# Strassen-type products inside the first MLP stage of an attention and MLP kernel on one Trainium2 core

## The chip, the cores and the metric

The kernel runs on one core of one Trainium2 chip. The metric is the device time of one execution in microseconds. The core's engines that matter here: TensorE (PE in the profile, with its weight loads as PEld), VectorE (DVE), ScalarE (ACT), GpSimd (POOL) and SyncE (SP), whose queue starts most of the DMA transfers. TensorE's results go to PSUM banks; everything else that it reads lies in SBUF.

## What is computed

```
q, k, v: (4, 8, 768, 64) float32; proj (64, 6); w_in (512, 2048); w_out (2048, 512); alpha (2048)

bucket = sum((x @ proj > 0) * 2**bit)                  # for q and for k
mask   = q_bucket[..., :, None] == k_bucket[..., None, :]
scores = where(mask, q @ k.T / 8, -1e9)
attn   = softmax(scores) @ v                           # (4, 8, 768, 64)
x = attn.transpose(0, 2, 1, 3).reshape(3072, 512)
h = x @ w_in
g = maximum(h, 0) + alpha * minimum(h, 0)
out = g @ w_out                                        # (3072, 512) float32
```

## The kernel before

The kernel first runs the attention of all 16 pairs of heads, and then, batch by batch, the MLP: for each of the four batches a first stage (w_in and the activation) and a second stage (w_out). All matrix products of the MLP are float32, and TensorE makes each of them in two passes, so that a product over one block of 128 rows of K is two entries in the trace.

**Seven products in place of eight.** The first stage of a batch computes the transpose of h, 2048 rows (features) by 768 columns (tokens), as a product of w_in's transpose with x's transpose. It is split in two along the features, along K (2 x 256) and along the tokens (2 x 384 columns; `CW` is 384), and the resulting 2x2 by 2x2 product is made with seven partial products (Strassen's method, in Winograd's form) over sums and differences of quarters. The sums of w_in's quarters were made during the attention and lie in DRAM as `w_in_s`: for each block i seven matrices m = 0 to 6, of two K blocks each. The sums of x's quarters are `x_m[b, 0..6]`, of which 3, 5, 4 and 6 are made by VectorE from the loaded quarters 0, 1, 2 and 5 (`sum_x`, 128x768 each).

**A block.** `ff1(b, i)`, i = 0 to 7, makes 128 features of each feature half: a `Product` with seven steps. Step n multiplies one of the seven matrices with one of the seven x's, into one of three PSUM banks a, b, c:

| step | matrices (w, x) | bank | what follows |
|---|---|---|---|
| 1 | 0, 0 | a, new | ScalarE copies a into bank b (the seed of b; in block 0 into SBUF as `p1`) |
| 2, 22 | 1, 1 | b, adds to the seed | quarter "11" is done: ScalarE copies it into SBUF as `h`, VectorE applies the activation |
| 5 | 3, 3 | c, new | ScalarE keeps c as `p5` |
| 6 | 4, 4 | a, adds | ScalarE keeps a as `u1` |
| 3 | 6, 2 | c, new | VectorE adds `u1` and c: quarter "12", activation |
| 7 | 5, 5 | a, adds | ScalarE keeps a as `u2`; VectorE adds `p5` and `u2`: quarter "22", activation |
| 4 | 2, 6 | a, adds | quarter "21": ScalarE copies it as `h`, VectorE applies the activation and makes four differences of g |

Each of those products is two matrix multiplications of 128x128 by 128x384 (two K blocks). Banks a come from `two_banks`, three buffers of two banks each that all stages share in turn; b and c are one bank each. Step 1 of the next block is put before step 4 of the present one, so the order on TensorE is, for block i: 1 of i, 4 of i-1, 2, 5, 6, 3, 7, then 1 of i+1.

**The second stage** (`ff2`) is built the same way with two levels: seven outer products n (in the order 1, 2, 5, 6, 3, 7, 4), each of them a `Product` of seven with 192 columns (`HC`) and four K blocks. VectorE makes the inner sums of w_out (`sum_w2`, tiles ws3 to ws6 from the loaded tile `wl`) and of g (`sum_g2`, tiles gs3 to gs6) as they are needed. The outer products are added up in the tiles m, m1 and m5, turned by VectorE (`turn_out`, two transposes each) and stored by twelve DMAs on SyncE's queue.

**Order.** `do` (`keep_in_program_order`) lets every computing instruction stand on its engine where the code has it; the DMAs that aren't pinned may be placed earlier. The loop over `blocks` runs through the batches: eight blocks of the first stage, seven of the second. In it, `load_w` asks for the first stage's matrices three blocks ahead, `load_x` and `sum_x` prepare the next batch's x during the second stage (the sums in its last block, n = 6), and `largest` and `verdict`, a check of the value ranges, run in the first stage of batch 1.

**Where a wait arises.** Dependencies between engines are kept by tile. A buffer that is given out again waits for all that used it before, and a two-bank tile counts as one tile.

Of the kernel before, what the change touches and what calls it, by code (L numbers as in the profile page):

```python
# [8 lines left out]
F32 = mybir.dt.float32  # L9
# [398 lines left out]
def fast_path(  # L408
# [13 lines left out]
    P = 128  # L422
# [52 lines left out]
    w_out_r = dram.tile([4, P, NI, DM // 2], F32, name="w_out_r")  # L475
    w_out_s = dram.tile([4, P, NI, DM // 2], F32, name="w_out_s")
    x_s = dram.tile([B, NP, P, S], F32, name="x_s")
    NW = NK * NF // 2
    wmax = const.tile([P, NW], F32, name="wmax")

# [216 lines left out]
    def two_banks(name):  # L697
        return psum.tile([P, 2, 512], F32, name=name, tag="sc", bufs=3)
# [167 lines left out]


    x_m, w_m, g_m = {}, {}, {}

    def pinned(when, ins):  # L870

# [90 lines left out]
                self.finish("21", self.ps["a"], None)  # L962

    def ff1(b, i):
        def finish(c, t, more):
            if more is None:
                h = mid.tile([P, CW], F32, name=f"h{b}_{i}", tag="h")
                do(ACT.copy(h, t))  # L968
            else:
                h = t  # L970
                do(DVE.tensor_tensor(h, t, more, op=ALU.add))

            al = alpha[:, i + NI * (c[0] == "2") :][:, :1]
            m = {"11": 0, "21": 1, "22": 2, "12": 5}[c]
            do(DVE.scalar_tensor_tensor(new_g(b, m)[:, i], h, al, h, op0=ALU.mult, op1=ALU.max))  # L975
            if c == "21":

                for to, x, y in ((3, 5, 0), (5, 2, 5), (4, 2, 3), (6, 1, 4)):
                    do(DVE.tensor_tensor(new_g(b, to)[:, i], g_m[b, x][:, i], g_m[b, y][:, i], op=ALU.subtract))  # L979

        w = w_m[b * NI + i]
        return Product(
            f"f{b}_{i}", CW, 2, lambda m, k: w[:, m, k], lambda m, k: x_m[b, m][:, k], finish,
            seeded=("b",) if i else (),
        )

    def new_g(b, m):

# [7 lines left out]
    H2, HK, HC = DM // 4, NI // 2, CW // 2  # L996
    w2, g2, m2, to_turn = {}, {}, {}, []

    def load_w2(b, n):
# [289 lines left out]
    for j, (b, what, n) in enumerate(blocks):  # L1289
        n2 = n + 1 if what == "2" else 0 if n == NI - 1 else 7  # L1290
        if n2 == 0:
            sides_g(b, 0)
            sum_w2(b, 0, 3, 4)
        now.step(2) if j else now.step(6)
        if j == 0:
            now.step(3)
            now.step(7)
            now.step(2)
        now.step(22)
        if (b, what, n) == (1, "1", 1):  # L1300
# [21 lines left out]
        if what == "1":  # L1322
            load_w(b * NI + n + 3)

            if 0 <= n - NI + (4 if b else 2) < 2:
                load_w2(b, n - NI + (4 if b else 2))
        else:
            load_w2(b, n + 2)
            if b + 1 < B:
                if n == 0:  # L1330
                    load_x(b + 1)
                if n == 6:
                    for m in range(4):
                        sum_x(b + 1, m, DVE)
        if j + 1 < len(blocks):
            turn_out()
        else:
# [38 lines left out]
```

## Time and profile before

| | |
|---|---|
| runs | 868.88, 869.24, 870.54 us; median 869.24 |
| profiled execution | 869.49 us, its span (first to last instruction) 867.7 us |
| busy in the span | PE 857.9, DVE 732.7, ACT 377.5, POOL 115.2 us |
| granted TensorE clock | 0.998 |
| attention and what lies before the MLP | to about 312 us |
| first stage of batches 1, 2, 3 | about 449 to 514, 587 to 652, 724 to 789 us |
| DMA | 135.4 MB, mean 156 GB/s |

The batches are counted from 0, as in the code. "Busy" counts the time in which at least one instruction of the engine runs, by the profile; the ends of matrix multiplications are modelled, and a row of several in a line of the timeline gives the start of the first and the time to the end of the last. In such rows the numbers of buffers and batches are left out: `f_3a` is bank a of block 3 in whichever batch, `z_4a` bank a of the second stage's outer product 4. What stands in brackets is the idle time before an instruction and what ended it. The page's part for the chain that ended last is empty for this kernel.

### The profile page before, as it was taken

Reading aid. Unit: us, or ns where it says so; the run is one execution under the profiler, and the core shown is the slowest. Engines: PE = TensorE matmul, PEld = TensorE weight load, DVE = VectorE, ACT = ScalarE, POOL = GpSimd, SP = SyncE. Lnnn points to the kernel's source line nnn. Section 1 sums busy time; section 2 is a strip of 40 time slices with the busy share of each in tenths; the row PEclk is TensorE's granted clock in tenths of the full one; section 3 lists DMA queues with packets and bytes.
Section 4 is the critical chain, followed back from the end, with each engine's and each line's share of the span. In section 5 each row is a group of like instructions: output and inputs, shape, how many; then the busy total and the mean of one; then the engine's idle time right before and its main releaser. Section 6 shows DMA issues by size and latency. Waiting matters only on the chain.

```text
span 867.7 us, 14629 instructions
## 1 busy us (share of the span) xinstructions
PE 857.9 (99%) x5458; PEld 572.7 (66%) x5458; DVE 732.7 (84%) x1188; ACT 377.5 (44%) x682; POOL 115.2 (13%) x249
## 2 busy tenths in 40 slices
PE   9999999999999999999999999999999999999996
PEld 4444444444444445569985559996558997557996
DVE  6999999999999977899887669897669898668886
ACT  7777888877788823321113331112332112232111
POOL 1322423432433310210000000000000000000001
PEclk9999999999999999999999999999999999999999
DMA  8956879778697536775334444433425334420242
GB/s 204 189 130 134 209 179 232 173 200 235 132 265 198 158 131 235 258 280 191 116 115 122 138 153 133 144 127 90 173 86 182 129 108 130 149 85 1 97 164 60
DMA packets 171105, 135.36 MB, mean 156 GB/s; under 512 B 126240, under 2 KB 155088, under 8 KB 167440
## 3 DMA queue, kind: packets, MB, share of 16 engines
q1 hardware_dynamic: 158528, 108.44, 44.1%
q0 software_dynamic: 9488, 24.56, 9.5%
q10 hardware_dynamic: 3008, 1.33, 0.6%
q8 instruction: 45, 0.74, 0.4%
q14 instruction: 36, 0.29, 0.1%
HBM read 104.87 MB, written 28.31 MB: 153 GB/s over the span
## 4 chain that ended last, share of the span: by engine, by line


## 5 line engine op out<-in xcount | busy, mean ns | idle before, releaser
L786 PE MATMUL sc<-qT,kT 64*128 64x384 f32 x768 | 155.3, 483 | 0.0
L789 ACT ACTIVATE pt<-sc 128x768 f32<-128x768 f32 x192 | 153.9, 812 | 3.1 <-PE sc L786 2.8
L819 PE MATMUL av<-pt,vn 128*32 128x385 f32 (+1 forms) x1536 | 127.0, 486 | 0.0
L819 PEld LDWEIGHTS av<-pt,vn 128*32 128x32 f32 x1536 | 50.3, 109 | 73.8 <-issue 68.8
L786 PEld LDWEIGHTS sc<-qT,kT 64*128 64x128 f32 x768 | 68.5, 187 | 37.6 <-issue 37.3
L979 DVE TENSOR_TENSOR g<-g,g 128x384 f32<-128x384 f32 x128 | 68.3, 554 | 2.2
L1098 POOL DMA_DIRECT2D out_dram<-o x4 | 2.2, 555 | 474.2 <-DVE o L1091 474.2
L786 PE MATMUL sc<-qb,kb 64*128 64x384 bf16 x384 | 63.5, 324 | 0.5 <-ACT pt L789 0.3
L975 DVE SCALAR_TENSOR_TENSOR g<-h,alpha 128x384 f32<-128x384 f32 x60 | 36.8, 614 | 25.2 <-ACT h L968 25.1
L1036 DVE TENSOR_TENSOR ws<-wl 128x512 f32<-128x512 f32 x56 | 38.5, 687 | 22.1 <-DMA wl<-w_out_s 18.9
L1044 DVE TENSOR_TENSOR gs<-g,gs 128x768 f32<-128x768 f32 x56 | 53.3, 952 | 1.0
L1044 DVE TENSOR_TENSOR gs<-g 128x768 f32<-128x768 f32 x56 | 53.2, 951 | 0.0
L786 PEld LDWEIGHTS <-kb 64*128 64x128 bf16 x384 | 19.8, 94 | 34.4 <-issue 11.5
L606 ACT ACTIVATE wr<-raw 128x512 int32<-128x512 uint32 x32 | 22.2, 693 | 30.4 <-DVE wso L650 15.2
L797 DVE TENSOR_TENSOR accp<-pt,pt 128x1536 f32<-128x1536 f32 x16 | 28.1, 1756 | 7.2 <-ACT pt L789 7.2
L747 POOL DMA_DIRECT2D qb<-hr x60 | 30.0, 507 | 26.4 <-ACT hr L742 26.4
L802 DVE TENSOR_TENSOR accd<-accd,pt 128x1536 f32<-128x1536 f32 x16 | 28.1, 1759 | 1.7
L808 DVE TENSOR_TENSOR accd<-accd,accp 128x1536 f32<-128x1536 f32 x16 | 28.1, 1758 | 0.6
L805 DVE TENSOR_TENSOR accp<-accp,pt 128x1536 f32<-128x1536 f32 x16 | 28.0, 1752 | 0.0
L801 DVE TENSOR_TENSOR accd<-pt,pt 128x1536 f32<-128x1536 f32 x16 | 28.0, 1751 | 0.0
L1248 ACT ACTIVATE qT<-qT 128x768 f32<-128x768 f32 x15 | 12.7, 845 | 25.1 <-DMA kb<-hr 20.6
L919 PE MATMUL f_0a<-x,wi 128*128 128x384 f32 x64 | 23.5, 491 | 0.0
(366 smaller groups left out, 1760.6 us busy)
## 6 DMA issues: line engine op xcount, KB each, us to landing
wi<-w_in_s SPq DMA_DIRECT2D x32, 896.0 KB
wl<-w_out_s SPq DMA_DIRECT2D x16, 1024.0 KB
wl<-w_out_r SPq DMA_DIRECT2D x12, 1024.0 KB
raw<-in_moe_w_in_dram POOLq DMA_DIRECT2D x15, 512.0 KB, 5.0
raw<-in_moe_w_out_dram POOLq DMA_DIRECT2D x14, 512.0 KB, 4.7
w_in_s<-wsi SPq DMA_DIRECT2D x16, 448.0 KB
qn<-in_q_dram SPq DMA_DIRECT2D x64, 96.0 KB
vn<-in_v_dram SPq DMA_DIRECT2D x16, 384.0 KB
```

Of the source, the lines that this page charges most:

```text
L747: queue.dma_start(bits[name, pi][D * s : D * s + 2 * NB, half * CW : (half + 1) * CW], raw[c : c + 2 * NB],)
L786: do(PE.matmul(sc[:, s, :CW], what["k", pi][r, ks], what["q", pi][r, qs], start=first, stop=not first,))
L789: do(ACT.activation(pts[kc][:, g, :, :CW], sc[:, :, :CW], AF.Exp, scale=SCALE / DOWN))
L797: do(DVE.tensor_tensor(accp[pi], p(0), p(1), op=ALU.add))
L801: do(DVE.tensor_tensor(accd[pi], p(3), p(4), op=ALU.add))
L802: do(DVE.tensor_tensor(accd[pi], accd[pi], p(5), op=ALU.add))
L808: do(DVE.tensor_tensor(accd[pi], accd[pi], accp[pi], op=ALU.add))
L819: do(PE.matmul(av[pi][D * s + t : D * s + t + 32, g, :w], nat["v", pi][:, s, kc * D + t : kc * D + t + 32], pts[kc][:, g, s, :w], start=(k ...
L975: do(DVE.scalar_tensor_tensor(new_g(b, m)[:, i], h, al, h, op0=ALU.mult, op1=ALU.max))
L979: do(DVE.tensor_tensor(new_g(b, to)[:, i], g_m[b, x][:, i], g_m[b, y][:, i], op=ALU.subtract))
L1036: do(DVE.tensor_tensor(t, w2[b, n, x], w2[b, n, y], op=op))
L1044: do(DVE.tensor_tensor(t, g2[b, n, x], g2[b, n, y], op=ALU.subtract))
```

## The change

In batches 1 to 3 two of the seven partial products of each block, 1 and 5 (matrices 0, 0 and 3, 3), are no longer made block by block. For four blocks together (a "unit", u = 0 or 1: 512 features, K of 256, 384 columns) each of the two is split once more in half along all three dimensions and made with seven smaller products (`Inner`, o = 0 for product 1 and o = 1 for product 5), each of two features blocks of 128x128 by 128x192. Their results lie in SBUF tiles `n_s`. The blocks themselves (`Rest`) make the other five products, and ScalarE copies the inner results into the banks a, b and c before the products that add to them.

Within an `Inner` of unit 1, ScalarE copies bank a into bank b, and the sum of b's two products into `n_s`; in unit 0 the sum is made by VectorE. The two `Inner` of a unit are interleaved by hand in `unit`, with the last step of the block before and the first steps of the unit's first block.

The sums that the inner products need are made by VectorE: those of x for each batch (`sum_inner_x`, three instructions each for o = 0 and 1), those of w_in in batch 1 only (`sum_inner`, four each), from where they are stored to DRAM (`w_n_s`) and loaded in batches 2 and 3 (`load_inner`, which also loads the plain quarters once more). Three of the four `sum_x` of these batches move from the second stage's end into unit 0, and the fourth to its last block but after other sums. `largest` and `verdict` move to the second stage of batch 1. In a `Rest`, steps 1 and 2 of the next block both stand before step 4 of the present one.

```diff
@@ -962,6 +964,8 @@
                 self.finish("21", self.ps["a"], None)
 
     def ff1(b, i):
+        whole = b == 0
         def finish(c, t, more):
             if more is None:
                 h = mid.tile([P, CW], F32, name=f"h{b}_{i}", tag="h")
@@ -979,10 +983,191 @@
...
         w = w_m[b * NI + i]
-        return Product(
-            f"f{b}_{i}", CW, 2, lambda m, k: w[:, m, k], lambda m, k: x_m[b, m][:, k], finish,
-            seeded=("b",) if i else (),
+        kind, seeded = (Product, ("b",) if i else ()) if whole else (Rest, ("a", "b", "c") if i else ("a",))
+        made = kind(
+            f"f{b}_{i}", CW, 2, lambda m, k: w[:, m, k], lambda m, k: x_m[b, m][:, k], finish, seeded=seeded,
         )
+        if not whole:
+            made.p1, made.p5 = (n_s[b, i // 4, o, i % 4 // 2][:, i % 2] for o in range(2))
+        return made
+    class Rest(Product):
+        def seed(self, bank, what):
+            t = two_banks(self.name + bank)[:, 0] if bank == "a" else psum_bc[0].tile([P, 512], F32, name=self.name + bank, tag=bank)
+            self.ps[bank] = t[:, : self.width]
+            do(ACT.copy(self.ps[bank], what))
+        def step(self, n):
+            if n == 1:
+                self.seed("a", self.p1)
+                if "b" in self.seeded:
+                    self.seed("b", self.p1)
+            elif n == 22 and "b" not in self.seeded:
+                self.finish("11", self.p1, self.ps["b"])
+            elif n == 5:
+                if "c" in self.seeded:
+                    self.seed("c", self.p5)
+            elif n == 3 and "c" not in self.seeded:
+                self.times("c", 6, 2, True)
+                do(DVE.tensor_tensor(self.sb["u1"], self.sb["u1"], self.p5, op=ALU.add))
+                self.finish("12", self.sb["u1"], self.ps["c"])
+            elif n == 6:
+                self.times("a", 4, 4, False)
+                self.keep("a", "u1")
+            elif n == 7:
+                self.times("a", 5, 5, False)
+                self.keep("a", "u2")
+                self.finish("22", self.p5, self.sb["u2"])
+            else:
+                super().step(n)
+    n_w, n_x, n_s = {}, {}, {}
+    QUADS = {0: (0, 0), 1: (0, 1), 2: (1, 1), 21: (1, 0)}
+    def load_inner(b, u):
+        t = late[0].tile([P, NI, 2 * P], F32, name=f"wn{b}_{u}", tag="wl")
+        blocks = t[:, :4].rearrange("p i (k f) -> p i k f", k=2)
+        nc.sync.dma_start(blocks, w_in_s[4 * u : 4 * u + 4, :, 0].rearrange("i p k f -> p i k f"))
+        if b > 1:
+            nc.sync.dma_start(t[:, 4:], w_n_s[u, 0])
+        for m, (f, kh) in QUADS.items():
+            n_w[b, u, 0, m] = blocks[:, 2 * f : 2 * f + 2, kh]
+        for m in range(4):
+            n_w[b, u, 0, 3 + m] = t[:, 4 + m].rearrange("p (t f) -> p t f", t=2)
+        for f in range(2):
...
+    def sum_inner(b, u, o):
+        if b != 1:
+            return
+        for m, x, op, y in ((3, 21, ALU.add, 2), (4, 3, ALU.subtract, 0), (5, 0, ALU.subtract, 21), (6, 1, ALU.subtract, 4)):
+            do(DVE.tensor_tensor(n_w[b, u, o, m], n_w[b, u, o, x], n_w[b, u, o, y], op=op))
+            nc.gpsimd.dma_start(w_n_s[u, o, :, m - 3].rearrange("p (t f) -> p t f", t=2), n_w[b, u, o, m])
+    def sum_inner_x(b, o):
+        x = x_m[b, 3 * o]
+        if o == 0:
+            t = mid.tile([P, 4, HC], F32, name=f"xn{b}_0", tag="x", bufs=1)
+        else:
+            t = late[0].tile([P, 4, HC], F32, name=f"xn{b}_1", tag="gs5", bufs=1)
+        left, right = (x[:, :, c * HC : (c + 1) * HC] for c in range(2))
+        do(DVE.tensor_tensor(t[:, :2], right, x[:, 0].rearrange("p (c w) -> p c w", c=2), op=ALU.subtract))
+        do(DVE.tensor_tensor(t[:, 2], right[:, 1], t[:, 0], op=ALU.subtract))
+        do(DVE.tensor_tensor(t[:, 3], left[:, 1], t[:, 2], op=ALU.subtract))
+        n_x[b, o] = {0: left[:, 0], 1: left[:, 1], 2: right[:, 1], 3: t[:, 0], 4: t[:, 2], 5: t[:, 1], 6: t[:, 3]}
+    class Inner:
+        TAGS = ({"p1": "h", "p5": "p1", "u1": "p5", "u2": "ws5"}, {"p1": "h", "p5": "ws6", "u1": "m1", "u2": "gs6"})
+        def __init__(self, b, u, o, a, b_, c):
+            self.key, self.o, self.seeded = (b, u, o), o, u > 0
+            self.name = f"n{b}_{u}_{o}"
+            self.ps = {"a": a, "b": b_, "c": c}
+            self.sb = {}
+            for f in range(2):
+                n_s[b, u, o, f] = late[0].tile([P, 2, CW], F32, name=f"{self.name}_{f}", tag=f"gs{3 + f}", bufs=2)
+        def times(self, bank, left, right, start):
+            b, u, o = self.key
+            for t in range(2):
+                first = start and t == 0
+                do(PE.matmul(
+                    self.ps[bank][:, t * HC : (t + 1) * HC], n_w[b, u, o, left][:, t], n_x[b, o][right],
+                    start=first, stop=True, skip_group_check=not first,
+                ))
+        def bank(self, name):
+            return self.ps[name][:, :CW].rearrange("p (t w) -> p t w", t=2)
+        def to(self, f, c):
+            b, u, o = self.key
+            return n_s[b, u, o, f][:, :, c * HC : (c + 1) * HC]
+        def keep(self, bank, what):
+            tag = self.TAGS[self.o][what]
+            home = mid if tag in ("h", "p1", "p5") else late[0]
+            more = {} if tag == "h" else {"bufs": 1}
+            t = home.tile([P, CW], F32, name=self.name + what, tag=tag, **more)
+            do(ACT.copy(t, self.ps[bank][:, :CW]))
+            self.sb[what] = t.rearrange("p (t w) -> p t w", t=2)
+        def step(self, n):
+            if n == 1:
+                self.times("a", 0, 0, True)
+                if self.seeded:
+                    do(ACT.copy(self.ps["b"][:, :CW], self.ps["a"][:, :CW]))
+                else:
+                    self.keep("a", "p1")
+            elif n == 5:
+                self.times("c", 3, 3, True)
+                self.keep("c", "p5")
+            elif n == 2:
+                self.times("b", 1, 1, not self.seeded)
+                if self.seeded:
+                    do(ACT.copy(self.to(0, 0), self.bank("b")))
+                else:
+                    do(DVE.tensor_tensor(self.to(0, 0), self.sb["p1"], self.bank("b"), op=ALU.add))
+            elif n == 6:
+                self.times("a", 4, 4, False)
+                self.keep("a", "u1")
+            elif n == 3:
+                self.times("c", 6, 2, False)
+                do(DVE.tensor_tensor(self.to(0, 1), self.sb["u1"], self.bank("c"), op=ALU.add))
+            elif n == 7:
+                self.times("a", 5, 5, False)
+                self.keep("a", "u2")
+                do(DVE.tensor_tensor(self.to(1, 1), self.sb["p5"], self.sb["u2"], op=ALU.add))
+            elif n == 4:
+                self.times("a", 2, 6, False)
+                do(ACT.copy(self.to(1, 0), self.bank("a")))
+    def unit(b, u, before):
+        t, both = two_banks(f"na{b}_{u}"), two_banks(f"nb{b}_{u}")
+        one = Inner(b, u, 0, t[:, 0], both[:, 0], t[:, 1])
+        one.step(1)
+        one.step(5)
+        before.step(4)
+        one.step(2)
+        one.step(6)
+        if u == 0:
+            sum_inner(b, 0, 1)
+            for n in range(1, 4):
+                sum_x(b, n, DVE)
+        t = two_banks(f"nc{b}_{u}")
+        two = Inner(b, u, 1, t[:, 0], both[:, 1], t[:, 1])
+        two.step(1)
+        one.step(3)
+        two.step(5)
+        one.step(7)
+        two.step(2)
+        two.step(6)
+        one.step(4)
+        two.step(3)
+        now = ff1(b, 4 * u)
+        now.step(1)
+        two.step(7)
+        now.step(2)
+        two.step(4)
+        return now
 
...
@@ -1291,14 +1475,25 @@
         if n2 == 0:
             sides_g(b, 0)
             sum_w2(b, 0, 3, 4)
-        now.step(2) if j else now.step(6)
+        if not j:
+            now.step(6)
+        elif not (b and what == "1"):
+            now.step(2)
         if j == 0:
             now.step(3)
             now.step(7)
             now.step(2)
         now.step(22)
-        if (b, what, n) == (1, "1", 1):
+        if (b, what, n) == (1, "2", 1):
             largest()
+        if what == "2" and n == 6 and b + 1 < B:
+            load_inner(b + 1, 0)
+            sum_inner_x(b + 1, 0)
+            sum_x(b + 1, 0, DVE)
+        if b and what == "1" and n == 1:
+            load_inner(b, 1)
+        if b and what == "1" and n in (2, 3):
+            sum_inner(b, 1, n - 2)
         if 0 < n2 < 7:
             sides_g(b, n2)
             sum_w2(b, n2, 3, 4)
@@ -1312,7 +1507,7 @@
             now.step(7)
             sum_w2(b, n2, 5)
             sum_g2(b, n2, 5)
-        if (b, what, n) == (1, "1", 3):
+        if (b, what, n) == (1, "2", 3):
             verdict()
 
         for n_out in [(), (0,), (1,), (2, 3), (4,), (5, 6), (7,)][j] if j < 7 else ():
@@ -1330,8 +1525,8 @@
                 if n == 0:
                     load_x(b + 1)
                 if n == 6:
-                    for m in range(4):
-                        sum_x(b + 1, m, DVE)
+                    sum_inner(b + 1, 0, 0)
+                    sum_inner_x(b + 1, 1)
         if j + 1 < len(blocks):
             turn_out()
...
@@ -1339,9 +1534,16 @@
         before = now
         if j + 1 < len(blocks):
             b1, what1, n1 = blocks[j + 1]
-            now = ff1(b1, n1) if what1 == "1" else ff2(b1, n1)
-            now.step(1)
-        before.step(4)
+            if b1 and what1 == "1" and n1 % 4 == 0:
+                now = unit(b1, n1 // 4, before)
+            else:
+                now = ff1(b1, n1) if what1 == "1" else ff2(b1, n1)
+                now.step(1)
+                if b1 and what1 == "1":
+                    now.step(2)
+                before.step(4)
+        else:
+            before.step(4)
         if n2 < 7:
             sum_g2(b, n2, 6)
     turn_last(1)
```

The part of `load_inner` that is left out loads the plain quarters for o = 1 (tiles `wq`, two of 256 KB, in the buffers of the tiles m) and, in batches 2 and 3, their stored sums (tiles `wp`, in the buffers of ws3 and ws4).

More of the change, by code (lines that the diff above doesn't have):

```diff
@@ L477, in fast_path @@
     x_s = dram.tile([B, NP, P, S], F32, name="x_s")
+    w_n_s = dram.tile([2, 2, P, 4, 2 * P], F32, name="w_n_s")
     NW = NK * NF // 2
@@ L868, in fast_path @@
     x_m, w_m, g_m = {}, {}, {}
+    H2, HK, HC = DM // 4, NI // 2, CW // 2
     def pinned(when, ins):
@@ new lines, in fast_path @@
+    n_w, n_x, n_s = {}, {}, {}
[11 more added lines that the diff above has]
+        for f in range(2):
+            t = late[0].tile([P, 2, 2, P], F32, name=f"wq{b}_{u}_{f}", tag="m", bufs=3)
+            nc.sync.dma_start(t, w_in_s[4 * u + 2 * f : 4 * u + 2 * f + 2, :, 3].rearrange("i p k f -> p i k f"))
+            for m, (ff, kh) in QUADS.items():
+                if ff == f:
+                    n_w[b, u, 1, m] = t[:, :, kh]
+        for h in range(2):
+            t = late[0].tile([P, 2, 2 * P], F32, name=f"wp{b}_{u}_{h}", tag=f"ws{3 + h}", bufs=2)
+            if b > 1:
+                nc.sync.dma_start(t, w_n_s[u, 1, :, 2 * h : 2 * h + 2])
+            for m in range(2):
+                n_w[b, u, 1, 3 + 2 * h + m] = t[:, m].rearrange("p (t f) -> p t f", t=2)
+            n_w[b, u, h] = t
@@ L995, in fast_path @@
     SIDES = {1: (0, 0), 2: (1, 1), 5: (3, 3), 6: (4, 4), 3: (6, 2), 7: (5, 5), 4: (2, 6)}
-    H2, HK, HC = DM // 4, NI // 2, CW // 2
     w2, g2, m2, to_turn = {}, {}, {}, []
```

## The prediction

> **What bounds the kernel now.** I read the page's busy shares first, then the busy time by stage, then TensorE's waits, and then the instructions in order of time in the first MLP stage. The page and two stretches of the run (batch 2's first stage, then its second; columns: length, busy us and instructions of PE, PEld, DVE, ACT, POOL, granted clock, DMA share, GB/s):
>
> ```profile
> PE 857.9 (99%) x5458; PEld 572.7 (66%) x5458; DVE 732.7 (84%) x1188; ACT 377.5 (44%) x682; POOL 115.2 (13%) x249
> ```
>
> ```profile
> 587.00:652.00 65.00, 65.00 (x207) 38.80 (x206) 42.13 (x76) 19.95 (x42) 0.00 (x0) 1.00 0.36 117
> 652.00:724.00 72.00, 72.00 (x420) 68.58 (x419) 66.22 (x107) 13.70 (x40) 0.00 (x0) 1.00 0.45 145
> ```
>
> TensorE never stops in either; its list of waits names 2.5 us in the whole run, none in the first stage of batches 1 to 3. So a product saved is its time saved, but only as long as nothing makes TensorE wait. Why nothing does, the timeline of the first stage shows (start, length; x4 is two blocks of K in two passes each):
>
> ```profile
> 593.18 1.45 PE L919 MATMUL f_0a<-x,wi 128*128 128x384 f32 x4
> 594.47 1.46 PE L919 MATMUL f_1a<-x,wi 128*128 128x384 f32 x4
> 594.67 0.48 ACT L926 COPY f_0u<-f_0a 128x384 f32<-128x384 f32 x1 [2.10 <-DVE g L975]
> 595.76 1.45 PE L919 MATMUL f_0a<-x,wi 128*128 128x384 f32 x4
> 595.96 0.46 ACT L934 COPY f_1b<-f_1a 128x384 f32<-128x384 f32 x1 [0.81 <-PE f_1a L919]
> 597.05 1.45 PE L919 MATMUL f_1b<-x,wi 128*128 128x384 f32 x4
> ```
>
> A product takes a slot of 1.29 us. A copy starts 0.20 after its product's slot ends, and there is always another product between a copy and the product that needs it: the seed of f_1b is done at 596.42, its product starts at 597.05. A block of seven products is 9.03 us, a batch of eight 72.2.
>
> **What is saved.** The inner products are 192 wide, like those of the second stage:
>
> ```profile
> 578.93 1.46 PE L919 MATMUL z_4b<-g,wl 128*128 128x192 f32 x8
> 580.23 1.46 PE L919 MATMUL z_4c<-gs,ws 128*128 128x192 f32 x8
> ```
>
> Eight take 1.30 us, so an inner product (two blocks, two passes: four) takes 0.65. For four blocks the change drops 8 products of 1.29 (10.32) and adds 14 of 0.65 (9.10): 1.22 saved per unit, 7.3 us for six units. That is all there is to gain.
>
> **What a wait costs.** One place of the trace has TensorE waiting for a ScalarE copy:
>
> ```profile
> 318.16 0.47 ACT L926 COPY f_0u<-f_0a 128x384 f32<-128x384 f32 x1
> 318.68 0.94 PEld L919 LDWEIGHTS f_0a<-x,wi 128*128 128x128 f32 x4 [0.63 <-ACT f_0u L926]
> 320.08 1.45 PE L919 MATMUL f_0b<-x,wi 128*128 128x384 f32 x4
> ```
>
> It starts 0.05 after the copy's end, and its slot is 1.40 instead of 1.29: 0.11 for the restart. ScalarE's instructions in a row start 0.09 closer than they are long:
>
> ```profile
> 24.27 0.68 ACT L610 ACTIVATE wx<-raw 128x512 f32<-128x512 f32 x1
> 24.86 0.83 ACT L725 ACTIVATE qn<-qn 128x768 f32<-128x768 f32 x1
> ```
>
> A copy from SBUF into PSUM is in no row. Bounds: 0.46 (L934, into PSUM from PSUM), and 0.57, which is 0.48 times 0.69/0.58: the 512-wide activation from SBUF (L606, 0.69) over what the PSUM copies (0.318 at 192 columns, 0.478 at 384) give for 512. I take 0.46, the same width and target; at 0.57 each seed in a row adds 0.11.
>
> **From one block to the next inside a unit (18 places).** Of a block five products remain; order on TensorE: b, the last of the block before, a (step 6), c, a (step 7). On ScalarE the changed program's order is: keep u2, seed a, seed b of the next block. Keep u2 waits for step 7, and TensorE's very next product is that b. So all three copies stand between two neighbouring products: 0.20 + 0.39 + 0.39 + 0.46 + 0.05 + 0.11 = 1.60 us idle. Next, c: its seed stands on ScalarE behind the two h copies, of which the first waits for the old block's last product: done 0.20 + 0.39 + 0.39 + 0.46 + 0.05 = 1.49 after that, with one product of 1.29 in between: 0.20 + 0.11 = 0.31. Keep u1 and step 7 then fit. Period 5x1.29 + 1.91 = 8.36. VectorE needs 2x0.55 + 4x0.61 + 2.2 = 5.8 of it and delays nothing. 18x1.91 = **34.4**. Without the overlap of ScalarE's rows, 2.25 each; with copies of 0.38 in a row and no c wait, 1.3.
>
> **The second unit of a batch (3).** Counting from step 7's end of block 3: first inner product to 0.65; the copy into bank b is done at 1.31, and the second product, although in another bank, waits for it in the changed program (1.36 to 2.12); old block's last to 3.41; then inner 2, 6 to 4.71; the other half's 1 to 5.36; step 3 waits for u1 (5.39), to 6.20; 5 to 6.85; step 7 waits for VectorE's add (behind block 3's four g subtractions: 7.4), to 8.2; 2, 6, 4 to 10.15; 3 for u1, to 11.0; 7 again for VectorE's add, 11.9 to 12.6; b of block 4, inner 4, a to 15.85; c to 17.45 with its seed's wait; a to 18.75. Work in it: 14x0.65 + 5x1.29 = 15.55. So 3.2 idle, 3x: **9.6** (half to 1.2 times this).
>
> **The first unit of a batch (3).** There VectorE and SyncE come in. The four subtractions of x (0.87 each) move out of the end of the second stage into the unit, with six small ones for the inner sides (0.53+0.27+0.27, twice), and the product that uses bank "nc" waits for VectorE's last add on the old z bank, behind all this and two transposes (1.03). From step 7's end of the last z product (585.43 in the trace): VectorE gets there at 5.3. The weights of the second half (256 KB) are queued on SyncE behind twelve output DMAs:
>
> ```profile
> 581.90 14.90 SPq L1098 DMA_DIRECT2D out_dram<-o  x24
> ```
>
> 0.62 each, so issued about 589.7, 4.2 after that point; landing 1.2 to 4.8 later (a 1 MB load issued at 570.03 ended VectorE's wait at 575.04), say 2.6: 7.0. Inner 1 of the second half 7.0 to 7.8; 3 and 5 to 9.25; step 7 waits for VectorE (three x subtractions to 8.4, an add) to 9.3, then as above to 20.2 for the end of block 0: 4.6 idle. In batch 1 VectorE also makes the inner weights' sums itself (eight of 256 columns, 0.36 each, from 0.27 at 192 and 0.53 at 384), the first four ahead of inner step 5 (2.8 idle) and the rest ahead of the add that step 7 waits for (3.2), in all about 7.7. 7.7 + 2x4.6 = **16.9**, from 10 (DMA and VectorE in time) to 25 (landing at the upper end).
>
> What moves otherwise is covered: the safety check's few small instructions go to batch 1's second stage, where TensorE has products queued and VectorE has some 6 us in 72 left (uncovered, under 1 us). Extra loads are about 1.5 to 2 MB a unit against a DMA share of 0.36 in that stage; w_in for block 3 is still asked for some 14 us ahead.
>
> **Sum.** Profiled execution 869.5 (span 867.7, 1.8 around it, 0.25 above the median of the runs): 869.5 - 7.3 + 34.4 + 9.6 + 16.9 = 923.1. I say **923 us**. By bounds: 869.5 - 7.3 + 23 + 5 + 10 = 900, and 869.5 - 7.3 + 40 + 12 + 25 = 939; seeds at 0.57 besides, three in each of 18 places, 6 more: 945.
>
> [...] The clock is 1.00 in both stretches, with no gap to test it. [...]
>
> **Rivals.** (1) ScalarE's copies hide: had TensorE another product between keep u2 and the seeded b, 1.29 of the 1.60 would be covered, as 595.96 to 597.05 shows for the old seed. For it: ScalarE is busy only 20 of 65 us, so throughput is there. Against: the changed program's order has no product between. Then the 18 places cost 0.6 each and the sum is 869.5 - 7.3 + 11 + 9.6 + 16.9 = 900. (2) The saving wins: all seeds are ready on time, in the units too; 869.5 - 7.3 = 862. This decides as soon as idle time is under 7.3 us over 18 block changes and 6 units, 0.3 each, which is less than the 0.20 after a product plus one copy. (3) TensorE's granted clock drops in the gaps. A first stage holds 70 us of products a batch; a tenth of the clock is 21 us over three batches: some 944. For: gaps every 4 to 8 us, unlike anything in the trace. (4) The first units cost far more, since a weight load queued behind outputs lands late on SyncE: each further us there is 3 us; three more, 932.
>
> **Chances.** Forecast, with (4) as its upper part, 0.78; (1) or other cheaper copies 0.11; (3) 0.08; (2) 0.03. Range 902 to 945: it holds the forecast and (4), the upper edge of (1) and the lower of (3). Differences under 0.2% (1.7 us) can't be told from none here: faster by more 0.03, within 0.01, slower 0.96.
>
> **What would show it.** In the changed profile: in the first stage of batches 1 to 3 TensorE idle about 1.6 before each b product, released by ScalarE's seed; keep u2, seed a, seed b in a row on ScalarE; periods of 8.4 us; ten-odd us more per batch, batch 1 the longest; second stages unchanged at 66; TensorE near 93% busy; clock 1.00. The forecast is wrong if b starts without waiting for its seed, if the inner products aren't 0.65, or if the clock falls.

## The result, and the profile after

| | before | after |
|---|---|---|
| median of the runs | 869.62 us (868.88 to 870.75, six) | 931.36 us (930.53 to 933.21, six) |
| ratio | | 1.0711, 95% interval 1.0697 to 1.0724 |
| profiled execution, its span | 869.49, 867.7 | 931.16, 929.3 |
| granted TensorE clock | 0.998 | 0.996 |

The forecast of 923 lies 8 us under the measured time, inside its range. The page's busy line, then TensorE's list of waits (what waited, for whom; total, times, longest, us):

```profile
PE 871.6 (94%) x5602; PEld 588.8 (63%) x5602; DVE 760.2 (82%) x1255; ACT 410.6 (44%) x766; POOL 123.9 (13%) x265
```

```profile
PE na L1092 <- DVE n L1133: 5.7, 6, 2.7
PE nc L1092 <- DVE n L1133: 4.3, 6, 0.7
PE f_1b L921 <- ACT f_1b L999: 4.3, 3, 1.4
PE f_2b L921 <- ACT f_2b L999: 4.1, 3, 1.4
...
PE na L1092 <- DVE wn L1059: 2.8, 1, 2.8
PE z_2c L921 <- DVE m L1249: 2.3, 3, 0.8
```

L1092 is an inner product, L999 a seed copied from SBUF. Six rows like the one for f_1b stand there, 25 us in all; before, the whole list was 2.5. Where TensorE's idle time lies, two stretches of the after kernel show (batch 2's first stage, then its second; the columns as in the prediction):

```profile
608.71:698.20 89.49, 76.03 (x279) 47.86 (x278) 54.23 (x103) 32.71 (x74) 0.00 (x0) 1.00 0.45 142
698.20:763.48 65.28, 64.09 (x389) 63.02 (x388) 59.45 (x94) 11.49 (x35) 0.00 (x0) 1.00 0.45 145
```

In the first, TensorE works 76 of 89 us at full clock, and over the stage as a whole no other engine comes near its own limit: this is order, not throughput. In the second it is also idle for 1.2 us, and VectorE works 59.5 of 65.3. From the first products of each stage in the timeline:

| stage (us) | before | after | difference | forecast |
|---|---|---|---|---|
| first, batch 1 | 72.44 | 94.06 | +21.6 | +19.9 |
| first, batch 2 | 72.25 | 89.38 | +17.1 | +16.8 |
| first, batch 3 | 72.25 | 90.12 | +17.9 | +16.8 |
| second, batches 1, 2, 3 | 63.69, 63.69, 66.34 | 65.50, 65.39, 68.04 | +5.2 | 0 |
| up to batch 0's first product | 312.26 | 313.14 | +0.9 | 0 |
| second, batch 0 | 64.72 | 63.69 | -1.0 | 0 |

(The forecast's column is 2.4 saved, six waits of 1.91, and the units' 3.2 and 7.7 or 4.6; the last second stage is taken up to the last transposition.) With 0.1 less behind the last transposition these are the 61.6 that the span grew. The table ahead of the prediction ends the first stages too early: in the timeline of before they run from 449.3 to 521.7, 585.4 to 657.7 and 721.4 to 793.6. So the prediction's second stretch (652 to 724) also holds the end of a first stage; in batch 2's second stage alone (657.7 to 721.4) VectorE is busy 58.2 of 63.7 us.

The wait between two blocks, in the timeline of the after kernel:

```profile
516.73 1.45 PE L921 MATMUL f_4a<-x,wi 128*128 128x384 f32 x4
518.22 0.48 ACT L928 COPY f_4u<-f_4a 128x384 f32<-128x384 f32 x1 [2.42 <-PE f_4a L921]
518.59 0.49 ACT L999 COPY f_5a<-n 128x384 f32<-128x384 f32 x1
519.01 0.49 ACT L999 COPY f_5b<-n 128x384 f32<-128x384 f32 x1
519.55 1.56 PE L921 MATMUL f_5b<-x,wi 128*128 128x384 f32 x4 [1.36 <-ACT f_5b L999]
```

Keep u2, seed a and seed b stand in a row between two neighbouring products. The next b starts at 527.94, so the period is 8.39. The brackets give 1.36, but the product before is listed 0.16 beyond its slot of 1.29, and the slot after the wait is 1.39 instead of 1.29: 1.62 lost in all. (Waits are given as in the brackets from here on.)

### The profile page after: what moved, and what is told of

Its sections match the earlier page's. It is cut to its first block, busy times and chain, and to the rows that moved or that the text cites. A ratio compares the mean times of both kernels' runs of the same rounds, so it can differ in the third digit from the quotient of the medians.

```text
span 929.3 us, 15186 instructions
## 1 busy us (share of the span) xinstructions
PE 871.6 (94%) x5602; PEld 588.8 (63%) x5602; DVE 760.2 (82%) x1255; ACT 410.6 (44%) x766; POOL 123.9 (13%) x265
## 4 chain that ended last, share of the span: by engine, by line
## 5 line engine op out<-in xcount | busy, mean ns | idle before, releaser
L1220 DVE TENSOR_TENSOR ws<-wl 128x512 f32<-128x512 f32 x56 | 38.4, 685 | 16.7 <-DMA wl<-w_out_s 15.9
L1092 PE MATMUL na<-xn,wn 128*128 128x192 f32 x96 | 21.3, 346 | 11.4 <-DVE n L1133 5.7
L1092 PEld LDWEIGHTS na<-xn,wn 128*128 128x128 f32 x96 | 16.0, 193 | 14.9 <-DVE n L1133 7.4
```

The source lines that it names most:

```text
L1092: do(PE.matmul(self.ps[bank][:, t * HC : (t + 1) * HC], n_w[b, u, o, left][:, t], n_x[b, o][right], start=first, stop=True, skip_group_che ...
L1220: do(DVE.tensor_tensor(t, w2[b, n, x], w2[b, n, y], op=op))
```

## Experiments

All times are medians of two runs, but for the last two kernels (four each); two runs of one kernel lie up to 4.8 us apart, so smaller differences rest on the timelines. The kernel before took 869.1 to 870.3 (medians) beside them.

**The old block's last product between the seeds and b** (the first rival's condition).

```diff
                 now.step(1)
+                before.step(4)
                 if b1 and what1 == "1":
                     now.step(2)
-                before.step(4)
```

> Inside a unit, the old block's last product is put between the seeds and the seeded product b (as in the kernel before). Theory (ScalarE's queue between two neighbouring products): the last product now waits only for keep u2, 0.20 + 0.48 + 0.05 + 0.11 = 0.84 instead of 1.63, and the c seed gets a product more of time, so its 0.31 goes too; 18 places x 1.10 = 20 us less, about 911.5 us. Rival 1 of the prediction (1.29 of 1.60 covered): 18 x 1.29 = 23 less, 908. Rival (VectorE's or the DMA queues' load sets the pace of the blocks): no change, 931.

Measured: 911.26, ratio 1.0473 (1.0440 to 1.0506), 20.1 less than after. In its timeline b starts at once, and the wait left is that of the old block's last product for keep u2:

```profile
518.41 1.56 PE L921 MATMUL f_4a<-x,wi 128*128 128x384 f32 x4 [0.57 <-ACT f_4u L928]
519.81 1.45 PE L921 MATMUL f_5b<-x,wi 128*128 128x384 f32 x4
```

So the seeds do cost the time, by their place and not by ScalarE's load.

**The seeds ahead of the block.** Seeds a and b of the next block are issued before step 7 of the present one, in the 18 places.

```diff
             sum_w2(b, n2, 6)
+            ahead_of = None
+            if j + 1 < len(blocks):
+                b1, what1, n1 = blocks[j + 1]
+                if b1 and what1 == "1" and n1 % 4:
+                    ahead_of = ff1(b1, n1)
+                    ahead_of.step(1)
             now.step(7)
```

> Inside a unit, the seeds of a and b are issued before step 7 of the present block, so that keep u2 stands behind them on ScalarE. Theory: the wait for b goes altogether, the wait for c stays; 18 x 1.63 = 29 us less, 902 us, and blocks of 6.76 us. If VectorE (5.8 us a block) or the DMA queues set the pace: less than half of that, 917 or more.

Measured: 902.44, ratio 1.0372 (1.0306 to 1.0437). The wait for b is gone, that for c (0.21 and its restart) is left, the period 6.76.

**The seed of c right behind that of b**, before the two h copies; everything else as in after.

```diff
                 if b1 and what1 == "1":
                     now.step(2)
+                    now.step(5)
```

> Inside a unit, the seed of c is issued right after that of b, ahead of the two h copies; in a unit's first block ahead of one. Theory: the wait of 0.31 before c goes in 21 places, 6.5 us less, 925 us, the wait for b unchanged. If c's own wait only covers another one behind it: 931.

Measured: 926.37, ratio 1.0647 (1.0616 to 1.0678): 5.0 less. The first stages are 6.9 shorter, as expected, 0.31 of it in each second unit (18.43 for 18.74), whose block 4 waits for the same seed; the second stages are 2.4 longer.

**Both together.**

> Both good edits at once: the seeds of banks a and b of the next block go out before step 7 of the present one, and the seed of c right behind b's, before the h copies (in a unit's first block before its own h copy). If the waits at the 18 places are as the traces so far say (0.32 for c left in the version with only the first edit, period 6.76), a period becomes five products, 6.45, and the time 902.4 - 18 x 0.31 = 896.9, with the six units' waits and the clock dips of their gaps left as they are (some 27). Rival: the c seed only pushes the h copies back, VectorE's last activation comes late and the wait moves to u1's copy: 902.

Measured: 897.67, ratio 1.0321 (1.0277 to 1.0366). The period is now five products and nothing else:

```profile
514.61 1.45 PE L921 MATMUL f_5b<-x,wi 128*128 128x384 f32 x4
...
521.06 1.45 PE L921 MATMUL f_6b<-x,wi 128*128 128x384 f32 x4
...
527.51 1.45 PE L921 MATMUL f_7b<-x,wi 128*128 128x384 f32 x4
```

The 18 places are thereby measured by removal: 931.4 - 897.7 = 33.7, with the three second units' c waits (0.9) in it and batch 1's first unit 1.2 longer (a wait of 2.82 with half-speed slots behind it, which in after had none). The second stages are 2.4 longer than after's, 1.3 of it in batch 0, where VectorE waited 1.49 for a load of w_out. From the periods alone the places cost 18 x (8.40 - 6.45) = 35.

**The seed of a copied twice**, in the 18 places.

```diff
                 self.seed("a", self.p1)
                 if "b" in self.seeded:
+                    if int(self.name.split("_")[1]) % 4:
+                        do(ACT.copy(self.ps["a"], self.p1))
                     self.seed("b", self.p1)
```

> Inside a unit, the seed of bank a is copied twice, one ScalarE copy more ahead of the seed of b in each of the 18 places, nothing else. Theory: each is on the path with its full distance to the next instruction, 0.41 us; 18 x 0.41 = 7.4 more, 938.8 us. Rival (ScalarE has slack there, something else sets the pace): 931.

Measured: 957.99, ratio 1.101 (1.0978 to 1.1042), more than either theory. The waits grew as expected, from 1.36 to 1.88, 0.52 each or 9.4 together. Another 17 us are in the products behind them:

```profile
485.82 1.71 PE L921 MATMUL f_2b<-x,wi 128*128 128x384 f32 x4 [1.88 <-ACT f_2b L999]
487.32 2.77 PE L921 MATMUL f_1a<-x,wi 128*128 128x384 f32 x4
489.88 1.77 PE L921 MATMUL f_2a<-x,wi 128*128 128x384 f32 x4
```

The second product's slot is 2.56, twice the 1.29, and the granted clock of the whole run is 0.974. Such slots follow 11 of the 18 waits, 1.6 us each. In these places the third rival, a falling clock, is thus 0.5 us of wait away from the kernel as it is.

**Half a copy more**, to see where between 1.36 and 1.88 this begins: the second copy takes only the left 192 columns.

> In the 18 places the seed of a is followed by a second copy of its left 192 columns (the same values): a wait 0.2 to 0.3 longer than 1.36, between the 1.36 that never lowered the clock and the 1.88 that did in about two of three places. By the wait alone: 931.4 + 18 x 0.25 = 936, granted clock 0.996 as before. If the clock already falls at 1.6: up to 19 more, 955, with product slots of 2 to 2.6 after some of the waits.

Measured: 938.55 (ratio 1.0792, 1.0729 to 1.0854). The waits are 1.72, so 18 x 0.36 = 6.5 more was due, 937.9, and no slot behind any of the 18 is longer than its restart.

**Two waits around one product.** The order of the first experiment, with u2 kept three times and seed a written six times.

```diff
                 self.keep("a", "u2")
+                if int(self.name.split("_")[1]) % 4 != 3:
+                    for _ in range(2):
+                        do(ACT.copy(self.sb["u2"], self.ps["a"]))
...
+                        for _ in range(5):
+                            do(ACT.copy(self.ps["a"], self.p1))
```

> What lowers the clock: one long wait, or little work in a stretch of time? The order of the first experiment (the old block's last product between keep u2 and the seeded b), with the copy u2 made three times and the seed of a six times: two waits of about 1.3 on either side of one product of 1.4, each no longer than the 1.36 that never lowered the clock, together 2.7 idle in 4.1. By the waits alone 911.3 + 18 x (0.77 + 1.56) = 953, clock 0.996. If it is the share of idle time in a window of some 3 us, slots at half speed follow as in the kernel with the seed copied twice, and the time is 960 to 975.

Measured: 963.20, ratio 1.1075 (1.1027 to 1.1123), with the clock at 0.996. The waits came out longer than planned, since here the copies to one and the same tile start 0.51 apart instead of 0.41:

```profile
525.80 1.56 PE L921 MATMUL f_4a<-x,wi 128*128 128x384 f32 x4 [1.59 <-ACT f_4u L1026]
529.18 1.56 PE L921 MATMUL f_5b<-x,wi 128*128 128x384 f32 x4 [1.82 <-ACT f_5b L999]
530.57 1.45 PE L921 MATMUL f_5a<-x,wi 128*128 128x384 f32 x4
```

From these, 911.3 + 18 x (1.02 + 1.82 + 0.11) = 964: the time is all waits, and the product behind is back at 1.29. TensorE idles 3.4 of 4.8 us there, and no slot at half speed stands behind. Nor does the length of one wait decide alone. In the trace of after a wait of 2.80 (449.97 to 452.77) is followed by slots of 0.72 and 1.30, at full speed, while behind one of 2.72 (458.65 to 461.37) the granted clock is 0.50 for 3.41 us (461.59 to 465.01), its only fall while products run. Cut into stretches of 3.41 us counted from that fall, the trace has the 2.72 whole in the stretch before it and the 2.80 divided as 1.39 and 1.42; from the first product of the MLP to the last no other stretch has more than 1.42 of idle time. In the kernel with the seed of c behind that of b a wait of 2.91 lowers nothing; in two such stretches it is 1.69 and 1.22. That idle time counts by such stretches is an estimate from these waits; why the clock falls, no run shows. First a stretch of the kernel with the seed of a copied twice, with a whole wait of 1.88 in it, and the one behind it, at half clock; then those of the 2.91 and the one behind them (columns as in the prediction):

```profile
483.68:487.09 3.41, 1.53 (x5) 0.87 (x5) 2.06 (x4) 1.76 (x4) 0.00 (x0) 1.00 0.46 112
487.09:490.50 3.41, 3.41 (x6) 1.69 (x5) 0.00 (x0) 0.37 (x1) 0.00 (x0) 0.50 0.00 0
```

```profile
449.66:453.07 3.41, 1.72 (x11) 1.43 (x9) 3.24 (x9) 0.80 (x2) 0.00 (x0) 1.00 0.28 67
453.07:456.48 3.41, 2.19 (x13) 2.22 (x14) 3.20 (x11) 0.48 (x1) 2.04 (x4) 1.00 0.69 229
456.48:459.90 3.42, 3.42 (x21) 2.90 (x19) 3.39 (x10) 0.96 (x2) 1.21 (x4) 1.00 0.37 123
```

**GpSimd instead of VectorE** for the four subtractions of x and batch 1's eight weight sums of the first unit.

```diff
-            sum_x(b + 1, 0, DVE)
+            for m in range(4):
+                sum_x(b + 1, m, POOL)
...
-                    sum_inner(b + 1, 0, 0)
+                    sum_inner(b + 1, 0, 0, POOL)
```

> All four subtractions of x for the next batch, and batch 1's eight sums of inner weights of the first unit, are made by GpSimd instead of VectorE (same results, four subtractions of x issued at the start of the last product of the second stage). Theory: the first unit of a batch waits for VectorE's queue. Then in batch 1 the waits of 2.80 (for wn) and 2.72 (for VectorE's add) go, and the clock fall after them (1.7): 7.2 less; in batches 2 and 3 the 0.69 before the fourth inner product of the second half and part of 0.72: about 0.7 to 1.4 each. 931.4 - 7.2 - 2 = 922. Rival: the weights' load, which lands late behind the output transfers, ends the same waits: 929 or more, with waits for wq of 1.3 to 2.5 in all three first units. Second rival: GpSimd is the slower engine (1.28 for 128x512) and the weights' sums are late themselves: 931 or more.

Measured: 947.41, ratio 1.0893 (1.0808 to 1.0979), 16 more where 9 less was expected. The first units did get shorter: 24.89, 20.21 and 20.95 became 22.98, 19.80 and 18.57. In batch 2 little, since the weights' load then ended the wait (1.66 instead of 1.26): the fourth rival's transfer, which VectorE's queue had covered. But GpSimd does the x subtractions as soon as x is there, at the entry of the second stage, and while it does, VectorE, for which TensorE waits in that place, slows down (VectorE and GpSimd in the timeline):

```profile
553.58 0.68 DVE L1218 TENSOR_TENSOR ws<-wl,ws 128x512 f32<-128x512 f32 x1
554.77 0.62 DVE L979 SCALAR_TENSOR_TENSOR g<-n,alpha 128x384 f32<-128x384 f32 x1
555.21 8.63 POOL L891 TENSOR_TENSOR x<-x,x 128x768 f32<-128x768 f32 x4 [47.02 <-DMA x<-x_s]
555.30 2.31 DVE L1218 TENSOR_TENSOR ws<-wl 128x512 f32<-128x512 f32 x1
557.53 2.55 DVE L1226 TENSOR_TENSOR gs<-g 128x768 f32<-128x768 f32 x1
560.01 2.16 DVE L979 SCALAR_TENSOR_TENSOR g<-h,alpha 128x384 f32<-128x384 f32 x1
```

The same operations take 2.31 instead of 0.68 and 2.16 instead of 0.62, and z_1a waits up to 5.7 for gs. So VectorE's queue is a part of the first units' idle time (1.9 in batch 1, 0.4 in batch 2, 2.4 in batch 3), but GpSimd is no free engine to move it to.

**The last block whole again** (on the version with both seeds early): block 7 of each first stage makes seven products; the inner results for it are made and not used.

```diff
-        whole = b == 0
+        whole = b == 0 or i == 7
```

> On top of the kernel with both seeds ahead (897.7): the last block of each first stage is made of seven products again (its inner results are made and not used). Theory: TensorE waits at the entry of the second stage (z_1a for gs, z_2c for m; 5.1 in that kernel's list of waits) because VectorE has the same activations and sums for two products less of cover. Then these waits go and 3 x 2 products of 1.29 are added: 897.7 - 5.1 + 7.7 = 900.3. Rival: the backlog comes from earlier blocks, which have also five products instead of seven: the waits stay, 905.4.

Measured: 897.94, ratio 1.0325 (1.0295 to 1.0355). Both waits at the entry of the second stage are gone from the list. Of after, then of this kernel:

```profile
554.16 1.55 PE L921 MATMUL z_1a<-gs,wl 128*128 128x192 f32 x8 [0.40 <-DVE gs L1228]
...
557.79 1.57 PE L921 MATMUL z_2c<-gs,ws 128*128 128x192 f32 x8 [0.78 <-DVE m L1249]
```

```profile
545.38 1.46 PE L921 MATMUL z_1a<-gs,wl 128*128 128x192 f32 x8
546.68 1.46 PE L921 MATMUL z_2b<-g,wl 128*128 128x192 f32 x8
547.98 1.46 PE L921 MATMUL z_2c<-gs,ws 128*128 128x192 f32 x8
```

From the first z_1a to the last z_2a of batch 1, after takes 21.18 and this 19.49, 1.69 less. Six products (7.7) were added. Against the version that this one is made from, the first stages take 6.8 more and the second stages of batches 1 to 3 6.1 less, so in the last blocks the two saved products bought about 1 of their 7.7. (That the medians are as equal as they are is in part chance: batch 0's second stage, which the edit leaves alone, is 1.3 shorter here.)

**A better order in the units**, in three steps on the version with both seeds early. First: another product between each copy or add and the product that waits for it, the x subtractions behind the adds, and the first units' load on GpSimd's queue.

```diff
         one.step(1)
-        one.step(5)
         before.step(4)
+        one.step(5)
...
-        one.step(7)
         two.step(2)
+        one.step(7)
...
-        two.step(7)
         now.step(2)
+        two.step(7)
+        now.step(22)
+        now.step(6)
         two.step(4)
```

> On top of the kernel with both seeds ahead (897.7): the order inside a unit gets another product between a copy or a VectorE add and the product that waits for it (the old block's last product before the first half's step 5, the second half's step 2 before the first half's 7, b and the first a product of the new block on either side of the second half's 7 and 4), the x subtractions stand behind the adds that TensorE waits for, batch 1's second four weight sums are split in two pairs, and the first unit's weights of the second half are asked for on GpSimd's queue instead of behind the output transfers on SyncE's. If the units' idle time is nothing but order (3.2 in each second unit, 4.6 in the first ones, 7.7 and 1.7 of clock fall in batch 1's): second units keep about 0.9, first ones 1.5, batch 1's 4: 7 + 6 + 5 = 18 less, 880. Rival: VectorE's queue is simply full there and the waits only move to later products: 890 to 898.

Measured: 887.63, ratio 1.0207 (1.0142 to 1.0272): 10 less, not 18. The first units took 21.07, 17.86 and 20.13; the second ones didn't get shorter (18.99 and 18.54 for 18.43), since block 4's own seeds were now late (0.71 and 0.95). And in batches 2 and 3 the second half's first product now waits for VectorE's add on the old z bank (1.14 and 1.92, the latter with slots at half speed behind it), so there the rival holds: the wait was passed on.

Second: block 4's seeds b and c as soon as their half is there, the sums of w_out for the second stage's first product one block earlier, VectorE's transposes later.

```diff
+        if u:
+            now.seed("b", now.p1)
         one.step(4)
...
+            if b and what == "1" and n == 5:
+                sum_w2(b, 0, 3)
+            if b and what == "1" and n == 6:
+                sum_w2(b, 0, 4, 6)
```

> How far order alone carries the idea. On top of the reordered units (887.6): in the second unit of a batch the seeds of block 4 go to their banks as soon as their half is there (b after the second half's step 6, c before its step 7), which should take the waits of 0.71 and 0.95 for f_4b and f_4c: 3 x 1.8 = 5.4; the product that needs no weight sum (the first half's step 2) runs before the one that does, and the second inner x sums and the two transposes stand behind the add that frees bank nc: the waits of 1.14 and 1.92 for m and the clock fall after the latter (1.6), and 0.65 of batch 1's 2.70, with its fall if the wait stays under 1.9: 6 to 7; the weights' sums for the first product of the second stage are made one block earlier, which should take the entry waits (4.3 in the list and some 0.5 of restarts). All of it: 887.6 - 5.4 - 6.5 - 4.8 = 871, within a us or two of the kernel before. Rival: VectorE, some 90% busy in those stretches, passes the delay on: 878 to 886.

Measured: 878.72, ratio 1.0100 (1.0083 to 1.0117), 9 less and not 16.7, inside the rival's 878 to 886. The entry waits are gone from the list, the second units take 16.99. What the transposes gave was lost again where they went (1.8 for the second half's step 7, three times).

Third: these behind the add, and the first half's steps 5 and 2 back in their order but for batch 1's first unit.

```diff
+            sum_x(b, 0, DVE)
             sum_inner_x(b, 1)
...
-            turn_out()
-            sum_x(b, 1, DVE)
             sum_x(b, 2, DVE)
...
-            sum_x(b, 3, DVE)
+            sum_x(b, 1, DVE)
...
+            turn_out()
+            sum_x(b, 3, DVE)
```

> The last waits of the version of 878.7: the second half's 7 waits 1.8 for an add that stands on VectorE behind two transposes and two x subtractions (3 x 1.8), these go behind it; the first half's 6 waits 0.6 for a copy in each unit (6 x 0.6) since its step 2 was moved ahead of 5, this is taken back but for batch 1's first unit; the first x subtraction stands no longer ahead of batch 1's weight sums (0.9 of 1.3). With a restart of 0.1 at each: 5.4 + 3.5 + 0.9 + 0.9 = 10.7 less, 868. That would be as good as the kernel before (870.1) or 0.2% better: nearly all of the 7.3 still goes into restarts. Rival: the adds come from a full VectorE and wait elsewhere, 872 to 876.

Measured: 877.16, ratio 1.0098 (1.0081 to 1.0114), 9 more than expected and hardly to be told from the step before, though the profiled span is 3.4 shorter (874.3). The units are 7.1 shorter, but the blocks behind them give half of it back, in waits for f_3b and f_1b that weren't there before, and the first subtraction of x now ends a wait in each first unit. TensorE's whole list of waits but for what the attention has:

```profile
PE nc L1094 <- DVE x L891: 3.2, 3, 1.7
PE f_3b L921 <- DMA wi<-w_in_s: 1.3, 1, 1.3
...
PE f_3b L921 <- ACT f_2u L928: 1.1, 2, 0.6
PE f_1b L921 <- ACT f_1b L999: 1.0, 3, 0.3
PE na L1094 <- ACT n_0u L1111: 0.6, 1, 0.6
```

That is 7.2. The units take 18.90, 16.34, 17.23, 16.33, 17.22 and 16.34 where their products are 15.55: 9.1 over, more than the 7.3 that the change can save. In the second units no wait is listed any more; their 0.8 is in slots like these:

```profile
492.58 0.81 PE L1094 MATMUL nc<-x,wq 128*128 128x192 f32 x4
493.32 0.92 PE L1094 MATMUL na<-x,wn 128*128 128x192 f32 x4
494.07 0.85 PE L1094 MATMUL nc<-xn,wp 128*128 128x192 f32 x4
```

Slots of 0.74 and 0.75 instead of 0.65: a product of 0.65 is a little short to cover a copy of 0.48 with its 0.20 before and 0.05 after, and each time the restart comes on top. No version here beats the kernel before.

## Why the prediction was right

**The saving: right, and small.** Inner products take 0.65 and the others 1.29, as said; the period falls to 6.45 where nothing waits.

**The wait between blocks: right**, in mechanism and size. 8.39 to 8.42 for the 8.36 forecast, with seeds of 0.49 where 0.46 was taken, 0.41 apart; 33.7 by removal and 35 from the periods, against 34.4.

**The second units: right**, 18.74 for 18.75, although each wait in it was worked out from bounds; the reordered kernels show that this idle time was order.

**The first units: right in batch 2, too small in the others.** Batch 2 took 20.21 for 20.15, in part by luck: the load came 0.8 us earlier than forecast (6.2 after the last z product, not 7.0), but the add of VectorE behind it came when forecast (9.2 for 9.3), so the total didn't change. In batch 1, 24.89 for 23.25: the term lacked the clock, which falls to 0.50 for 3.41 us behind a wait of 2.72 for VectorE (timeline of after):

```profile
457.73 0.92 PE L1092 MATMUL nc<-xn,wp 128*128 128x192 f32 x4
461.37 1.47 PE L1092 MATMUL na<-xn,wn 128*128 128x192 f32 x4 [2.72 <-DVE n L1133]
462.63 1.49 PE L1092 MATMUL nb<-x,wq 128*128 128x192 f32 x4
463.91 1.36 PE L1092 MATMUL nc<-xn,wp 128*128 128x192 f32 x4
465.10 0.81 PE L1092 MATMUL na<-xn,wn 128*128 128x192 f32 x4
```

Slots of 1.26, 1.28 and 1.19 instead of 0.65: 1.8 lost. The prediction's 7.7 for this unit holds idle time alone. In batch 3, 20.95 for 20.15: the second half's first product waited 1.41 for VectorE to free its bank, where the forecast had the load, and VectorE's next add came later too (a wait of 1.25 for 0.69 in batch 2).

**The second stages: wrong.** "Second stages unchanged at 66" is the step that failed; they grew by 1.7 to 1.8 each, 5.2 of the 8 missed; the first units are most of the rest. VectorE's 5.8 us a block were set against the period of 8.36 and found to fit, but the stage's end wasn't looked at: the last block's activations and differences stand together with the first sums for the second stage, and there are now two products less to cover them. With seven products in that block the waits vanish, and with the sums made a block earlier too. (The sign "ten-odd us more per batch" didn't fit the prediction's own sum of 17 to 20 either; it was 19 to 23.)

**The rivals.** (1) was right under its condition: 20.1 for 23, since the product between brings its own wait for keep u2 (0.57). (2) would have needed what three rounds of reordering didn't reach. (3) doesn't happen behind the 18 waits of 1.36 to 1.42 in after, and does behind 11 of the 18 of 1.88 to 1.94. (4) is real, 1.26 in batch 2, but VectorE is about as late there, so it adds little.

**The clock: right in the 18 places.** The runs show no slot at half speed behind any of 90 waits of 1.36 to 1.82 in the 18 places of four kernels, and such slots behind 11 of 18 from 1.88 to 1.94. The 0.996 of after, where 1.00 was said and before had 0.998, has one fall of 3.41 us while products run, behind the wait of 2.72 in batch 1's first unit. So waits of 1.36 left the clock alone, but with half a us to spare.

## What to carry to other kernels

Before a product is replaced by a copy into its bank, count what the product was covering: the copies of its neighbours and VectorE's work up to the next stage; here 1.22 saved per four blocks stood against 1.9 of uncovered copies at each of three block changes. An engine that is 44% busy can still stop TensorE if three of its instructions stand in a row between two products; issuing them earlier gave back 34 of the 62 us, with no work added. A wait can cost more than its length: here none of 90 waits of 1.36 to 1.82 us was followed by products at half speed, but 11 of 18 waits of 1.88 to 1.94 were, at another 1.6 us each.

## What was not expected of the hardware

- In the trace of after the granted clock falls to 0.50 for 3.41 us behind a wait of TensorE of 2.72. Slots at half speed stand behind 11 of 18 waits of 1.88 to 1.94 (the seed of a copied twice) and behind none of 90 from 1.36 to 1.82 in four kernels, but not behind one of 2.80 in after either, nor behind one of 2.91 in the kernel with the seed of c behind that of b.
- In the kernel with GpSimd instead of VectorE, while GpSimd subtracts x (555.21 to 563.84), three of VectorE's instructions take 2.7 to 3.5 times as long as the same operations before it (0.62 to 2.16, 0.68 to 2.31, 0.95 to 2.55), 1.5 to 1.6 longer each. Why, no run shows.
- In the trace of after ScalarE's copies of 128x384 from SBUF into PSUM take 0.49 and start 0.41 apart into different tiles; in the kernel with two waits around one product they start 0.51 apart when they write the same tile again.
